# Attention with a gated feed-forward, one core: two constants of the order planner, the sorting of the value groups, and when a group is summed from four copies

## The chip, the core and the metric

The kernel runs on one core of a Trainium2 chip. The metric is the device time of one execution in microseconds (us). Before the change the median of three runs is 769.64 us (769.48 to 770.63).

Five engines work side by side, each with its own queue of instructions, and meet at semaphores: TensorE (PE: matmuls, and PEld: the loading of their weights), VectorE (DVE), ScalarE (ACT), GpSimd (POOL, used only for set-up here) and SyncE (SP, which issues nearly all transfers).

## What is computed

```python
def reference(A_x, A_wqkv, A_wo, B_x, B_w_gate, B_w_up, B_w_down, gate_w):
    x = A_x                                          # 1 x 2048 x 512
    g = _sigmoid((x * gate_w).sum(-1, keepdims=True))
    a = _A_ref(x, A_wqkv, A_wo)                      # attention, 32 heads of 16
    b = _B_ref(x, B_w_gate, B_w_up, B_w_down)        # (silu(x @ w_gate) * (x @ w_up)) @ w_down, width 1792
    return g * a + (1 - g) * b
...
        scores = jnp.einsum("bhqd,bhkd->bhqk", q, k) * (Dh ** -0.5)
        p = _softmax(scores, axis=-1)
        o = jnp.einsum("bhqk,bhkd->bhqd", p, v)
```

Both halves take the same x. All tensors are bf16. The attention has 32 x 2048 x 2048 scores, and an exponential is due for each of them.

## The kernel before

**Tiles.** The queries are cut into 4 blocks of 512, the heads into 8 groups of 4; a block with a group is a unit (32 units, `UNITS`). A unit has 16 key tiles of 128 keys. One key tile of one unit, called a value group `n` here, is 4 heads x 128 keys x 512 queries of scores: 4 matmuls make the scores, their exponentials are taken, and they are multiplied with the values into the PSUM bank `o_ps` of the unit. There are 512 value groups.

**Two ways to take the exponential.** (1) On ScalarE: `emit_pair` (L704) issues two score matmuls into a two-bank tile `s_t`, of which there are two, and one ACT instruction on 128x1024 elements writes `e_t` (10 buffers). Two such pairs make a group. (2) On VectorE: `emit_d` (L774) issues one score matmul into `d_t`, one of three single PSUM banks that it shares with all projections. DVE scales the scores and adds a constant so that the 16-bit result, read as bf16, is a rough exponential (`first`). Four such tiles make the group's 128x2048 tile `y`. The rough exponential is then made better in one of two ways:

- *four summed* (`groups[n] == 4`): three copies of `y`, shifted by constants (`copy`, L816 and after), so that four tiles are multiplied with the values and TensorE's accumulation sums them. DVE does 4 + 3 instructions, TensorE 4 multiplications with the values.
- *two with a product* (`groups[n] == 2`): two bit operations (`bits`) and a multiplication of two 128x2048 tiles (`product`); two tiles are multiplied with the values. DVE does 4 + 2 + 1 instructions, TensorE 2 multiplications with the values.

The tiles `y` and their copies live in 7 homes (`NS`; they are named `c_t`, and the seventh lies in `wd_t` or `kaug` while these are free, so it goes by those names).

**The planner.** The order of every instruction on PE, DVE and ACT is written out by the program as it is built (`ordered` ties each instruction behind the one before on its engine). A planner decides it. It keeps a clock for each engine (`plan.pe`, `plan.dve`, `plan.act`) with a price for each step: an ACT tile 0.9167 us, a round of TensorE 0.217 us, a change between its row-tiled and column-tiled forms 0.107 us, a DVE step some 0.6 us. A round is one of four matmuls that lie side by side in columns of the array (all projections, all multiplications with the values), or the two to four score matmuls that lie side by side in rows. The main loop (L1491) fills the room until the next score tile is free with multiplications with the values (`pv`, from `pv_list`), with pieces of the projections and of the feed-forward (`side`), and, where nothing is left, with time that is counted as spare; then it emits a score pair, on which up to two `d_t` matmuls ride. Some pieces that remain are issued after the last score pair, by `tail_ready` (L1042). `next_pv` forces a multiplication with the values when too many pairs wait (`EB`).

**What the change touches.** `m_free` (L361) says when a single bank can be written again after DVE's read: 0.2 us after the planner's end of that read. The end of `emit_d` (L807) says when DVE can read a `d_t`: 0.28 us after the planner's end of the matmul. `ready` (L813) appends a finished tile of a DVE group to the list `vready`, and `pv_list` (L1330) offers them in that order. `pv` (L902) charges TensorE's clock with the multiplication, from time 0.0 for a DVE tile, that is, without regard to when the tile is ready. `quad` (L1469) chooses how a new DVE group is made: with the product if fewer than two homes (`FREE4`) are free or have a known time of coming free; otherwise four summed if over 0.5 us of TensorE's time has been spare since the last such choice, or if `EAGER` says so; with the product otherwise. `EAGER` is given `back[0]`, the number of ScalarE pairs whose multiplication with the values is still to come. It always says no.

Of the kernel before, what the change touches and what calls it, by code (L numbers as in the profile page):

```python
# [79 lines left out]
def kernel(  # L80
# [215 lines left out]
    plan = Plan()  # L296
    owed = []
    work_at = []
    banks = [0.0] * 3
    held = [None] * 3  # L300

    def spend(mode, mms, ready=0.0):

        plan.seq += 1
        work_at.append((plan.pe, mms))
        plan.pe = max(plan.pe + (FLIP if mode != plan.mode else 0.0), ready) + (0.226 if mode == "F" else 0.217) * mms
        plan.mode = mode
# [16 lines left out]
    def pay(i=0):  # L324
        ready, cost, f, c, key = owed.pop(i)
        spend_v(cost, ready, key)
        keep, plan.chain = plan.chain, None
        f()
        plan.chain = keep
        if c is not None:  # L330
            c.owed -= 1
            if c.done():
                c.done_at = plan.slot
# [14 lines left out]
    def m_tile(name, ride=None):  # L348
        while m_ready() is None:
            stuck()  # L350
        i = min((i for i in range(3) if banks[i] is not None), key=lambda i: banks[i])
        if ride is None:
            plan.pe = max(plan.pe, banks[i])
        else:
            ride.append(max(plan.pe - ROUND, banks[i]) + ROUND)
            plan.pe = max(plan.pe, ride[0])
        banks[i] = None
        held[i] = ps_m[i].tile([P, QBW], F32, tag=f"m{i}", name=name)
        return held[i]

    def m_free(ps, t):  # L361
        i = [h is ps for h in held].index(True)
        banks[i], held[i] = t + 0.2, None

    def emit_piece(c):
        mms, f = c.pieces[c.i][:2]
# [317 lines left out]
    vready = []  # L684
# [4 lines left out]
    def score(ps, b, rows=64):  # L689
        n, j = b // 4, HEADS[b % 4]  # L690
        (qb, g), kt = UNIT[n // KT], n % KT
        r = slice(32 * j // rows * rows, 32 * j // rows * rows + rows)
        q = (q0a if n < KT // 2 else q0[qb])[r, j % 2, :] if g == 0 else get_q(qb, g)[r, j % 2, :]
        mm(ps, lhsT=kaug[r, g, kt * P:(kt + 1) * P], rhs=q, start=True, stop=True,
           tile_position=(r.start, 0))
# [4 lines left out]
    e_end = {}  # L700
# [38 lines left out]
    d_wait = []  # L739
# [15 lines left out]
    def take_home():  # L755
        i = min(range(NS), key=lambda i: c_free[i])
        t, c_free[i] = c_free[i], 1e9
        assert t < 1e9
        users[i] = [1, 0.0]
        return i, t  # L760

    def home(i=None, t=0.0):

        if i is None:
            i, t = take_home()
        plan.dve = max(plan.dve, t)
        if i < NS - 1:
            return i, vex.tile([P, NV * QBW], U16, tag=f"h{i}", name="c_t", bufs=1)[:, :]
        return i, (kaug[:, 0, :] if au > QB else wd_t[:, 0:4, :].rearrange("p f d -> p (f d)")).bitcast(U16)
# [4 lines left out]
    def emit_d(i, rows=32, riding=False):  # L774
        if not vcur:
            n = v_take()
            waiting[n] = [NV, None, take_home()]
            vcur.update(n=n, left=list(range(NV)), y=None)
            y_live[0] += 1
        n, left, cur = vcur["n"], vcur["left"], waiting[vcur["n"]]  # L780
        left.remove(i)
        end = []
        d_t = m_tile("d_t", end if riding else None)
        score(d_t[:, :], 4 * n + i, rows)
        if not left:
            vcur.clear()

        def first():
            if cur[1] is None:
                cur[1] = home(*cur[2])  # L790
            h, y = cur[1]
            vec.tensor_scalar(out=y[:, i * QBW:(i + 1) * QBW], in0=d_t[:, :], scalar1=EXP_A, scalar2=EXP_B[groups[n]],
                              op0=ALU.mult, op1=ALU.add)
            m_free(d_t, plan.dve)
            cur[0] -= 1
            if cur[0]:
                return
            plan.last = ("y", n)
            if groups[n] == 2:
                vops.extend([(0.6, lambda: bits(n, 0, y), ("y", n), n, True), (0.6, lambda: bits(n, 1, y), None, n, True),  # L800
                             (MUL_US, lambda: product(n, h, y), None, n, False)])
            else:
                users[h][0] = 2
                ready(n, 0, h, y)
                for k in range(1, 4):
                    vops.append((0.6, lambda k=k: copy(n, k, h, y), ("y", n) if k == 1 else None, n, True))
        d_wait.append(((end[0] if end else plan.pe) + 0.28, first, n))  # L807

    waiting = {}
    copies = {}  # L810
    part = {}

    def ready(n, k, h, c):  # L813
        copies[n, k] = (c.bitcast(BF16), h)
        vready.append((plan.dve + 0.3, n, k))

    def copy(n, k, i, y):
        h, c = home()
        vec.tensor_scalar(out=c, in0=y, scalar1=SHIFTS[k - 1], scalar2=None, op0=ALU.add)
        ready(n, k, h, c)  # L820
        if k == 3:
            drop(i, plan.dve + 0.2)
            y_live[0] -= 1

    def bits(n, k, y):
        h, c = home()
        if k == 0:
            vec.tensor_scalar(out=c, in0=y, scalar1=0x007F, scalar2=0x3F00, op0=ALU.bitwise_and, op1=ALU.bitwise_or)
            part[n] = (h, c)
        else:  # L830
            vec.tensor_scalar(out=c, in0=y, scalar1=0xFF80, scalar2=None, op0=ALU.bitwise_and)
            ready(n, 0, h, c)

    def product(n, h, y):
        i, c = part.pop(n)
        vec.tensor_tensor(out=c.bitcast(BF16), in0=y.bitcast(BF16), in1=c.bitcast(BF16), op=ALU.mult)
        ready(n, 1, i, c)
        drop(h, plan.dve + 0.2)
        y_live[0] -= 1
# [62 lines left out]
    def pv(n, k=None, most=QBW):  # L902

        un = n // KT
        c0 = cut.pop("done", 0)
        c1 = min(QBW, c0 + most)
        cols = slice(c0, c1)
        if un not in o_of:
            while un and un - 1 not in osbs:
                pay()  # L910
            plan.pe = max(plan.pe, o_end[0])
            o_of[un] = ps_o.tile([P, QBW], F32, tag="o", name="o_ps")
        if v_of(n) is not None:
            force(v_of(n))
        o = o_of[un]
        first = pvs[un] in ((0, KT // 2) if un == 0 else (0,))
        last = un == 0 and pvs[un] == KT // 2 - 1 or pv_left(un) == 1
        if k is not None:
            c, slot = copies[n, k]
        for i, b in enumerate(range(4 * n, 4 * n + 4)):  # L920
            j = HEADS[i]
            v0 = (4 * UNIT[un][1] + j) * VC
            e = e_of[b] if k is None else c[:, i * QBW:(i + 1) * QBW]
            mm(o[32 * j:32 * j + 32, cols], lhsT=vaug[:, n % KT, v0:v0 + 32], rhs=e[:, cols],
               start=first, stop=last, tile_position=(0, 32 * j), skip_group_check=True)
        share = (c1 - c0) / QBW
        if c1 < QBW:
            cut.update(item=(n,) if k is None else (n, k), done=c1)
            spend("C", share, 0.0 if k is not None else max(e_end[b] for b in range(4 * n, 4 * n + 4)))
            return  # L930
        cut.clear()
        if k is not None:
            copies.pop((n, k))
        else:
            for b in range(4 * n, 4 * n + 4):
                e_of.pop(b)
                e_left.pop(b, None)
        pvs[un] += 1
        if un == 0 and pvs[0] == KT // 2:
            later(0.6, take_part, plan.pe + 0.47)  # L940
        spend("C", share, 0.0 if k is not None else max(e_end.pop(b, 0.0) for b in range(4 * n, 4 * n + 4)))
        if k is None:
            done_a[un] += 1
        else:
            done_v[un] += 1
            drop(slot, plan.pe + 0.2)
# [257 lines left out]
    for qb in range(1, QB):  # L1204
        d = qb * KT
        q, bd = q0_pieces(qb)
        q = pace.add(q, 0, d - 13, [known])
# [3 lines left out]
    for qb in range(QB):  # L1211
        for b in range(NB):
# [18 lines left out]
            q = pace.add(q_pieces(qb, b), rel, d - QLEAD, after)  # L1231
# [229 lines left out]
    def v_take():  # L1461
        un = v_unit()
        hi[un] -= 1
        n = un * KT + hi[un]
        groups[n] = 2 if quad() else 4
        forward()
        return n

    def quad():  # L1469
        if sum(f < 1e9 for f in c_free) < FREE4:  # L1470
            return True
        if spare[0] > SPARE or EAGER(len(GQL()), back[0]):
            spare[0] = 0.0
            return False
        return True
    FREE4 = 2
    EAGER = lambda q, b: False
    GQL = lambda: []
    back = [0]

# [10 lines left out]
    while au < UNITS:  # L1491
# [45 lines left out]
        n = au * KT + at_  # L1537
# [56 lines left out]
    for tq in range(TQ):  # L1594
        t = (QB - 1) * TQ + tq
# [39 lines left out]
```

## Time and profile before

| | us |
|---|---|
| median of three runs | 769.64 |
| the profiled execution, its own time | 769.63 |
| its span, from first to last instruction | 767.9 |
| start of the first ACT score tile (`e_t`) | 13.86 |
| start of the last one | 758.70 |
| ACT score tiles / `th` tiles of the feed-forward | 780 / 56 |

Busy shares of the span: PE 95%, DVE 96%, ACT 98%. The granted TensorE clock is 1.00 in all stretches. Read the profile so: the busy share of PE counts a matmul from its start to its modelled end, about 384 ns for 512 columns, though the next one starts after 0.22 us; so the starts of the matmuls in the timeline tell how much room PE has, and the busy share does not. The same holds in part for ACT and DVE: an ACT score tile is shown with some 1.1 us and the next one starts 0.90 us after it.

### The profile page before, as it was taken

How to read it: one execution, taken by the hardware profiler on the slowest of the kernel's cores; microseconds unless marked ns; L12 is line 12 of the kernel's file. 1: busy time of each engine (PE TensorE's matmuls, PEld its weight loads, DVE VectorE, ACT ScalarE, POOL GpSimd, SP SyncE). 2: the span in 40 equal slices, each digit the busy share in tenths (PEclk: the TensorE clock that was granted, in tenths of full speed). 3: DMA queues.
4: the chain of work that ended last, by engine and by line, in shares of the span. 5: the costliest groups of instructions: out<-in, count | busy, mean ns of one | idle time of the engine just before them, and what ended most of it. 6: DMA issues, size and time to landing. Idle time of an engine off the chain costs nothing.

```text
span 767.9 us, 22047 instructions
## 1 busy us (share of the span) xinstructions
PE 733.1 (95%) x9044; PEld 221.6 (29%) x9045; DVE 738.8 (96%) x1213; ACT 752.5 (98%) x849; POOL 10.6 (1%) x25
## 2 busy tenths in 40 slices
PE   8999999999999999999999999999999999999997
PEld 3323222222222222223322222223222322222222
DVE  6889999999999999999999999999999999999994
ACT  5999999999999999999999999999999999999996
POOL 5000000000000000000000000000000000000000
PEclk9999999999999999999999999999999999999999
DMA  8002304134200113220100230311000232100001
GB/s 192 2 5 50 73 15 85 31 107 101 57 19 13 32 24 78 60 52 22 37 26 12 49 84 20 75 34 41 20 12 26 60 77 59 31 16 16 16 28 35
DMA packets 91020, 34.38 MB, mean 45 GB/s; under 512 B 75488, under 2 KB 90472, under 8 KB 90920
## 3 DMA queue, kind: packets, MB, share of 16 engines
q1 hardware_dynamic: 89192, 32.66, 17.8%
q8 instruction: 70, 1.15, 0.6%
q10 hardware_dynamic: 1728, 0.33, 0.2%
q14 instruction: 30, 0.25, 0.1%
HBM read 21.55 MB, written 2.35 MB: 31 GB/s over the span
## 4 chain that ended last, share of the span: by engine, by line
ACT 32%; PE 30%; DVE 28%; issue 8%; DMA 1%; SPq 1%; DVEq 0%; ACTq 0%
ACT e_t L167 30%; DVE c_t L176 17%; PE s_t L164 10%; PE o_ps L164 8%; PE gu L164 6%; DVE kaug L176 3%; PE ops L164 3%; DVE mt L176 2%; DVE gs L176 2%; ACT th L167 1%; DVE on L176 1%; PE qp L164 1%; DVE osb L176 1%; PE warm L164 1%; SPq L176 1%
## 5 line engine op out<-in xcount | busy, mean ns | idle before, releaser
L167 ACT ACTIVATE e_t<-s_t 128x1024 bf16<-128x1024 f32 x780 | 728.3, 1105 | 1.3 <-PE s_t L164 0.7
L176 DVE TENSOR_SCALAR c_t<-d_t 128x512 uint16<-128x512 f32 x420 | 275.3, 681 | 2.2 <-PE d_t L164 2.0
L164 PE MATMUL s_t<-qx,kaug 32*128 32x512 bf16 (+1 forms) x1228 | 239.0, 384 | 16.1 <-ACT e_t L167 14.0
L164 PEld LDWEIGHTS <-kaug 32*128 32x128 bf16 (+1 forms) x2048 | 88.7, 91 | 321.8 <-issue 317.6
L164 PE MATMUL o_ps<-e_t,vaug 128*32 128x512 bf16 (+2 forms) x1608 | 154.2, 379 | 0.0
L176 DVE TENSOR_SCALAR c_t<-c_t 128x2048 uint16<-128x2048 uint16 x212 | 142.0, 683 | 1.7 <-PE o_ps L164 1.4
L164 PE MATMUL d_t<-qx,kaug 32*128 32x512 bf16 x404 | 131.9, 383 | 0.0
L164 PE MATMUL o_ps<-c_t,vaug 128*32 128x512 bf16 (+2 forms) x1244 | 111.3, 370 | 2.6 <-DVE osb L176 2.1
L164 PEld LDWEIGHTS <-vaug 128*32 128x32 bf16 x3048 | 68.8, 94 | 107.2 <-issue 95.2
L164 PE MATMUL gu<-xT,wg 128*32 128x512 bf16 x896 | 73.0, 384 | 0.0
L164 PE MATMUL gu<-xT,wu 128*32 128x512 bf16 x896 | 68.3, 382 | 0.2 <-DVE c_t L176 0.2
L176 DVE TENSOR_TENSOR c_t<-c_t 128x2048 bf16<-128x2048 bf16 x50 | 60.7, 1213 | 0.0
L164 PE MATMUL ops<-wd_t,mt 128*32 128x512 bf16 x672 | 57.5, 382 | 0.0
L164 PE MATMUL s_t<-q,kaug 32*128 32x512 bf16 (+1 forms) x196 | 38.2, 383 | 5.8 <-ACT e_t L167 5.4
L176 DVE TENSOR_SCALAR kaug<-d_t 128x512 uint16<-128x512 f32 x60 | 39.6, 680 | 0.0
L176 DVE SCALAR_TENSOR_TENSOR mt<-gs,gu 128x512 bf16<-128x512 bf16 x56 | 38.1, 680 | 1.5
L176 DVE SCALAR_TENSOR_TENSOR gs<-th,gu 128x512 bf16<-128x512 bf16 x56 | 38.0, 678 | 0.5 <-ACT th L167 0.5
L167 ACT ACTIVATE th<-gu 128x512 bf16<-128x512 f32 x56 | 37.7, 673 | 0.0
L164 PEld LDWEIGHTS <-mt 128*32 128x32 bf16 (+1 forms) x1037 | 24.5, 95 | 28.6 <-issue 22.0
L164 PEld LDWEIGHTS <-wu 128*32 128x32 bf16 x896 | 19.5, 95 | 25.4 <-issue 17.6
L164 PEld LDWEIGHTS <-wg 128*32 128x32 bf16 x896 | 17.8, 94 | 26.0 <-issue 23.2
L176 DVE TENSOR_SCALAR kaug<-c_t 128x2048 uint16<-128x2048 uint16 x33 | 22.5, 681 | 0.1
(141 smaller groups left out, 444.7 us busy)
## 6 DMA issues: line engine op xcount, KB each, us to landing
wg<-in_B_w_gate_dram SPq DMA_DIRECT2D x56, 128.0 KB
wu<-in_B_w_up_dram SPq DMA_DIRECT2D x56, 128.0 KB
on<-osb SPq DMA_DIRECT2D x120, 16.0 KB
rb<-rr SPq DMA_DIRECT2D x15, 128.0 KB
wd_t<-in_B_w_down_dram SPq DMA_DIRECT2D x7, 256.0 KB
qx<-qst SPq DMA_DIRECT2D x96, 16.0 KB
qx<-aq SPq DMA_DIRECT2D x96, 16.0 KB
out_dram<-o_t SPq DMA_DIRECT2D x12, 128.0 KB
```

Of the source, the lines that this page charges most:

```text
L164: return ordered(nc.tensor.matmul(*args, **kw))
L167: ordered(nc.scalar.activation(*args, **kw))
L176: return lambda *a, **kw: ordered(f(*a, **kw))
```

## The change

The two constants go from 0.2 to 0.14 and from 0.28 to 0.25. A new function `usable` keeps `vready` sorted by the time from which a tile is ready and notes that time; `pv` charges TensorE's clock for a DVE tile from that time on instead of 0.0. `EAGER` says yes where at most three ScalarE pairs wait.

```diff
     def m_free(ps, t):
         i = [h is ps for h in held].index(True)
-        banks[i], held[i] = t + 0.2, None
+        banks[i], held[i] = t + 0.14, None
...
-        d_wait.append(((end[0] if end else plan.pe) + 0.28, first, n))
-
+        d_wait.append(((end[0] if end else plan.pe) + 0.25, first, n))
+
+    def usable(t, n, k):
+        vready.append((t, n, k))
+        vready.sort(key=lambda v: v[0])
+        ready_at[n, k] = t
+
+    ready_at = {}
...
     def ready(n, k, h, c):
         copies[n, k] = (c.bitcast(BF16), h)
-        vready.append((plan.dve + 0.3, n, k))
+        usable(plan.dve + 0.3, n, k)
...
-            spend("C", share, 0.0 if k is not None else max(e_end[b] for b in range(4 * n, 4 * n + 4)))
+            spend("C", share, ready_at[n, k] if k is not None else max(e_end[b] for b in range(4 * n, 4 * n + 4)))
...
-        spend("C", share, 0.0 if k is not None else max(e_end.pop(b, 0.0) for b in range(4 * n, 4 * n + 4)))
+        spend("C", share, ready_at[n, k] if k is not None else max(e_end.pop(b, 0.0) for b in range(4 * n, 4 * n + 4)))
...
-    EAGER = lambda q, b: False
+    EAGER = lambda q, b: b <= 3
```

## Prediction, made before the changed kernel ran

> **What bounds the kernel now.** I read the page's totals first, then the busy time by stage, the waits of TensorE, and the timeline for the pace of each engine. From the page:
>
> ```profile
> PE 733.1 (95%) x9044; PEld 221.6 (29%) x9045; DVE 738.8 (96%) x1213; ACT 752.5 (98%) x849; POOL 10.6 (1%) x25
> ...
> L167 ACT ACTIVATE e_t<-s_t 128x1024 bf16<-128x1024 f32 x780 | 728.3, 1105 | 1.3 <-PE s_t L164 0.7
> L176 DVE TENSOR_SCALAR c_t<-d_t 128x512 uint16<-128x512 f32 x420 | 275.3, 681 | 2.2 <-PE d_t L164 2.0
> ...
> L176 DVE TENSOR_SCALAR c_t<-c_t 128x2048 uint16<-128x2048 uint16 x212 | 142.0, 683 | 1.7 <-PE o_ps L164 1.4
> ...
> L176 DVE TENSOR_TENSOR c_t<-c_t 128x2048 bf16<-128x2048 bf16 x50 | 60.7, 1213 | 0.0
> ```
>
> By stage (window; busy PE, PEld, DVE, ACT):
>
> ```profile
> 240.00:320.00 80.00, 77.15 (x952) 23.14 (x944) 79.86 (x129) 79.97 (x92) 0.00 (x0) 1.00 0.15 38
> 480.00:560.00 80.00, 78.04 (x974) 22.59 (x966) 79.76 (x128) 79.89 (x92) 0.00 (x0) 1.00 0.18 41
> ```
>
> and the waits of TensorE:
>
> ```profile
> PE s_t L164 <- ACT e_t L167: 20.3, 60, 0.7
> ...
> PE o_ps L164 <- DVE osb L176: 2.1, 5, 0.9
> ```
>
> ACT is the last limit: busy without a gap, and what TensorE waits for is ACT giving back a score tile. But three engines lie within a few per cent, so each one's real pace is needed. The timeline gives it by starts. TensorE:
>
> ```profile
> 301.62 0.40 PE L164 MATMUL o_ps<-c_t,vaug 128*32 128x512 bf16 x4
> 301.84 0.39 PE L164 MATMUL o_ps<-e_t,vaug 128*32 128x512 bf16 x4
> 302.17 0.39 PE L164 MATMUL s_t<-qx,kaug 64*128 64x512 bf16 x2
> 302.49 0.40 PE L164 MATMUL o_ps<-c_t,vaug 128*32 128x512 bf16 x4
> ```
>
> A column round after a column round: 0.22 us. A change to the score form: 0.33 and back 0.32. Over the whole trace the medians are 0.222 and 0.3215, so a change of form costs 0.10 on top of a round. DVE:
>
> ```profile
> 302.77 0.68 DVE L176 SCALAR_TENSOR_TENSOR gs<-th,gu 128x512 bf16<-128x512 bf16 x1
> 303.37 0.68 DVE L176 TENSOR_SCALAR c_t<-d_t 128x512 uint16<-128x512 f32 x1
> ...
> 308.09 1.22 DVE L176 TENSOR_TENSOR c_t<-c_t 128x2048 bf16<-128x2048 bf16 x1
> 309.22 0.68 DVE L176 SCALAR_TENSOR_TENSOR mt<-gs,gu 128x512 bf16<-128x512 bf16 x1
> ```
>
> One step is 0.60, a product 1.13. On ACT, 394 of the 721 intervals between neighbouring score tiles are 0.903 or 0.904 us, which is its own pace (0.9035); a `th` tile takes 0.477. From the first score tile's start (13.86) to the last one's (758.70) is 744.84 us; ACT's own need there is 779 x 0.9035 + 56 x 0.477 = 730.5. The difference, 14.3 us, is ACT starting late, nearly always because its score matmuls came late: call it ACT's loss, 0.018 us a tile.
>
> **The change, part by part.** The order of the two built programs, counted by operation, says what happens.
>
> *Groups.* DVE groups go from 122 to 124, so ACT tiles from 780 to 776: 4 x 0.9035 = 3.6 us less for ACT. Groups with a product go from 78 to 30, four summed from 44 to 94. DVE: 48 products less (48 x 1.13 = 54.2), bits and copies from 288 to 342 (54 x 0.60 = 32.4 more), 8 first steps more (4.8): 17.0 less. TensorE: value rounds for DVE groups from 78 x 2 + 44 x 4 = 332 to 30 x 2 + 94 x 4 = 436, for ACT's from 390 to 388, and 3 filler rounds fall away: 99 x 0.222 = 22.0 more; changes of form from 1500 to 1515, 1.5 more; 4 score pairs less, 0.9. Sum +22.6 us. Eight more `d_t` matmuls ride with score pairs and start within 0.01 us of them, at nothing. Transfers are the same in number; SP's queue only swaps weight loads with neighbours.
>
> *What TensorE's load does to ACT.* Priced with 0.222 and 0.10, TensorE's work up to the last score tile is 693.0 us before, 37.5 under ACT's 730.5, and 714.0 after (1.6 of the added work lies behind that tile), 12.9 under ACT's 726.9. That cover is what hides the added rounds; it is not gone, but thin. To see what thin cover costs I cut the program before into 49 windows of 16 score tiles and set each one's room (ACT's own need less TensorE's priced work, per tile) beside ACT's measured loss in it. Fifths by room: room 0.001, 0.027, 0.050, 0.071, 0.101 us; loss 0.0168, 0.0167, 0.0178, 0.0187, 0.0224. So loss did not grow as room fell, down to none. After, the mean room falls from 0.049 to 0.017; 22 of 49 windows are below zero, by 3.8 us in all, against 4 windows and 0.4 us. Where room is negative, the loss is at least the deficit, and a share of TensorE's stalls on DVE comes on top (all stalls in starts that a DVE read or write ended: 8.5 us, 0.011 a tile). Taking the larger of the usual 0.0175 and that floor, window by window, gives 1.7 us more than now; taking the fifths alone gives 0.8 less. I take +0.9, the nearer to the floor, since both are observed but the negative windows are new. Upper bound: deficits paid on top of the usual loss (3.8) with as much again from DVE stalls that no longer find cover: +7.6.
>
> *The Trainium skill on this.* "Perfetto Trace Analysis" (Identifying the Most-Contended Engine) holds that the busy time of matmuls is no measure of TensorE's headroom and that the busy share of weight loading is to be looked at instead. By that share, 29% here, TensorE would be far from a limit and the added 22.6 us would cost nothing. The starts above agree that 95% means little, but price 693.0 of 730.5 as taken, which is no headroom of 71%.
>
> *Constants and sorting.* The new values are what the trace has: a single bank is written again at the earliest 0.054 us after DVE's 0.68 us read ends, 0.135 after that read's pace of 0.60; DVE starts a `d_t` at the earliest 0.457 after its matmul's start, 0.24 after the 0.217 round. So nothing waits in principle, but a margin of 0.06 is gone: at 26 places where TensorE already stalls on such a bank it could cost 0.06 each, 1.6 us. Against that DVE is relieved by 17.0 us, and 1.6 us of ACT's loss stands behind a stall on DVE. The sorting and the honest charge in `pv` move multiplications off tiles that are not there yet; TensorE's waits for `c_t` sum to 1.3 us by starts. Bounds -1.6 to +1.6; I take -0.3, the relief being the larger row.
>
> *The end.* One thing in the new order is plain loss. A column tile of the output projection slips behind the last score pair: 28 matmuls, 7 rounds, stand now between it and the first matmuls of the tail. Before:
>
> ```profile
> 758.00 0.39 PE L164 MATMUL s_t<-qx,kaug 64*128 64x512 bf16 x2 [0.53 <-ACT e_t L167]
> 758.91 0.81 PE L164 MATMUL al<-wo_t,on 128*128 128x512 bf16 x2 [0.53 <-ACT e_t L167]
> 759.65 0.62 PE L164 MATMUL o_ps<-e_t,vaug 128*32 128x512 bf16 x8
> 760.32 0.69 ACT L167 ACTIVATE osb<-o_ps,tiny 128x512 bf16<-128x512 f32 x1 [0.54 <-PE o_ps L164]
> ```
>
> `al` waited for a score bank until 0.91 after the last score pair, and the last value round came when ACT's last tile was done. With 7 rounds ahead, `al` starts 0.32 + 7 x 0.222 + 0.10 = 1.97 after the pair: 1.06 later, and the rest of the tail hangs on it (value rounds, `osb`, denominators, output). Some of it hides only if TensorE is early at the pair, all 1.6 us of the rounds show if it is late; bounds 0.6 to 1.6; I take 1.1.
>
> Sum: 769.6 (the profiled execution, 769.63, equal to the median 769.64) - 3.6 + 0.9 - 0.3 + 1.1 = 767.7 us. About 0.2% (1.5 us, so 768.1 and 771.2) is what can be told from no change.
>
> **Rivals.**
>
> 1. *TensorE has headroom*: room never decides, ACT's loss goes by the fifths alone, and the relieved DVE stalls less. 769.6 - 3.6 - 0.8 - 0.3 + 1.1 = 766.0. For it: the flat loss in the fifths. Against: 22 windows where TensorE's priced work is over ACT's. (It is what the rule of the Trainium skill's "Perfetto Trace Analysis" named above would lead to.)
> 2. *The gain is eaten.* Each window with negative room pays its deficit on top of the usual loss: +3.8. 769.6 - 3.6 + 3.8 - 0.3 + 1.1 = 770.6, no change. For it: TensorE can only be one score tile ahead, so usual loss and deficit may add. Against: the lowest fifth shows no sum.
> 3. *Slower: TensorE becomes the bound in the second half.* In stretches of 48 score tiles TensorE's work now meets or passes ACT's at tiles 240-288 (44.0 us to 43.8), 384-480 (89.8 to 89.2) and 528-624 (88.4 to 88.1). There every stall on DVE is ACT's loss. It decides where room per tile is under those stalls, 0.011 us. Price +3.8 and, with all the stalls of the negative windows, +3.8 more: 774.4; with half of the latter 772.5. Against it: today TensorE waits for ACT's score tiles for 20.3 us by the page and 34.1 us by starts, and the added work is 22.6.
>
> That the groups do not change is excluded by the built order.
>
> **How the numbers follow.** Forecast 0.40 (its own range 766.8 to 768.9, a quarter of it within 0.2%), rival 1 0.12, rival 2 0.20, rival 3 0.28. Faster 0.30 + 0.12 = 0.42; the same 0.10 + 0.20 = 0.30; slower 0.28. The range takes rival 1 and most of rival 3, whose upper end is left out: 765.9 to 773.0.
>
> **What would show it.** Right: 776 score tiles at 0.9035; the waits of `s_t` for ACT down from 20.3 to some 5 to 10 us; PE busy near 750, DVE near 722; first to last score tile about 742; a run of 7 `ops` rounds behind the last score pair and `al` 2 us after it. Wrong: ACT idle on PE in the middle stretches, or a loss over 0.022 us a tile there (rival 3); a loss under 0.017 (rival 1); an end no longer than before.

## The result and the profile after

The changed kernel takes 766.74 us (median of 6 runs, 765.88 to 767.69) against 769.42 (6 runs, 769.09 to 770.63): ratio 0.9964, 95% interval 0.9951 to 0.9976. That is 2.7 us faster, clear of 0.2%; the forecast was 767.7. One execution of run e9 (1059.84 us at a granted clock of 0.56) and one of the kernel before beside it (2632.69 us) are left out below.

The two profiled executions, taken apart. *Need* is what ACT's tiles take at their own pace (0.9035 us from one score tile to the next, 0.477 for a `th`) between the starts of the first and the last score tile; *loss* is what that stretch takes beyond the need; *end* runs from the last tile's start to the last instruction.

| us | before | after | difference | forecast |
|---|---|---|---|---|
| start of the first score tile | 13.86 | 12.77 | -1.09 | 0 |
| ACT's need (780 and 776 tiles) | 730.5 | 726.9 | -3.6 | -3.6 |
| ACT's loss | 14.3 | 14.0 | -0.3 | +0.9 - 0.3 |
| end | 9.2 | 10.5 | +1.3 | +1.1 |
| span | 767.9 | 764.2 | -3.75 | |
| the execution's own time | 769.63 | 765.88 | -3.75 | |

The first line is not the change: up to there the two orders are the same, and in the profiled executions below, which share them too, the first tile starts anywhere from 12.4 to 13.9. Its size is about the gap between these two executions (-3.75) and the medians (-2.7).

The page after, in the lines that answer to those shown of before:

```profile
PE 742.6 (97%) x9472; PEld 218.8 (29%) x9473; DVE 725.0 (95%) x1227; ACT 748.5 (98%) x845; POOL 10.6 (1%) x25
...
L167 ACT ACTIVATE e_t<-s_t 128x1024 bf16<-128x1024 f32 x776 | 724.4, 1089 | 1.2 <-PE s_t L164 0.7
L176 DVE TENSOR_SCALAR c_t<-d_t 128x512 uint16<-128x512 f32 x444 | 292.8, 684 | 7.8 <-PE d_t L164 7.0
...
L176 DVE TENSOR_SCALAR c_t<-c_t 128x2048 uint16<-128x2048 uint16 x249 | 167.2, 685 | 0.7 <-PE o_ps L164 0.2
...
L176 DVE TENSOR_TENSOR c_t<-c_t 128x2048 bf16<-128x2048 bf16 x23 | 28.0, 1217 | 0.0
```

DVE is 13.8 us less busy and now waits for `d_t` (7.0 us) where it hardly did; TensorE is 9.5 us busier by records, although 22.6 us of work came by starts: the rest went into time that the records already counted. By stage, and in the waits of TensorE:

```profile
240.00:320.00 80.00, 79.58 (x1022) 22.63 (x1020) 79.62 (x135) 80.00 (x91) 0.00 (x0) 1.00 0.14 36
480.00:560.00 80.00, 78.66 (x1012) 22.86 (x1008) 78.25 (x132) 79.86 (x91) 0.00 (x0) 1.00 0.17 41
```

```profile
PE s_t L164 <- ACT e_t L167: 11.9, 35, 1.0
...
PE gu L164 <- DVE c_t L176: 0.5, 2, 0.3
```

ACT is as full as before. TensorE's waits for ACT fell from 20.3 to 11.9 us, and the 2.1 us for `osb` are gone. By starts, TensorE's stalls that ended with a read or write of DVE in the loop fell from 8.5 to 2.5 us.

The end of the changed kernel:

```profile
753.21 0.39 PE L164 MATMUL s_t<-qx,kaug 64*128 64x512 bf16 x2
...
753.53 1.70 PE L164 MATMUL ops<-wd_t,mt 128*32 128x512 bf16 x28
...
755.15 0.82 PE L164 MATMUL al<-wo_t,on 128*128 128x512 bf16 x2
...
756.58 0.69 ACT L167 ACTIVATE osb<-o_ps,tiny 128x512 bf16<-128x512 f32 x1 [1.85 <-PE o_ps L164]
```

The 28 `ops` matmuls (7 rounds) stand behind the last score pair, `al` starts 1.94 us after the pair (0.91 before), and ACT sits 1.85 us (0.54 before) until the last values are there.

### The profile page after: what moved, and what is told of

It reads as the page before. It is cut to its first block, busy times and chain, and to the rows that moved or that the text cites. A ratio compares the mean times of both kernels' runs of the same rounds, so it can differ in the third digit from the quotient of the medians.

```text
span 764.2 us, 22889 instructions
## 1 busy us (share of the span) xinstructions
PE 742.6 (97%) x9472; PEld 218.8 (29%) x9473; DVE 725.0 (95%) x1227; ACT 748.5 (98%) x845; POOL 10.6 (1%) x25
## 4 chain that ended last, share of the span: by engine, by line
PE 41%; ACT 37%; DVE 13%; issue 8%; DMA 1%; SPq 0%; ACTq 0%; DVEq 0%
ACT e_t L167 35%; PE s_t L164 14%; PE o_ps L164 13%; DVE c_t L176 7%; PE gu L164 5%; PE ops L164 3%; PE qp L164 2%; ACT th L167 2%; DVE mt L176 2%; DVE gs L176 1%; DVE kaug L176 1%; PE vp L164 1%; PE dps L164 1%; PE kp L164 1%; PE warm L164 1%
## 5 line engine op out<-in xcount | busy, mean ns | idle before, releaser
L176 DVE TENSOR_SCALAR c_t<-d_t 128x512 uint16<-128x512 f32 x444 | 292.8, 684 | 7.8 <-PE d_t L164 7.0
L164 PE MATMUL s_t<-qx,kaug 32*128 32x512 bf16 (+1 forms) x1224 | 238.2, 384 | 11.8 <-ACT e_t L167 10.8
L164 PEld LDWEIGHTS <-kaug 32*128 32x128 bf16 (+1 forms) x2048 | 81.9, 91 | 322.9 <-issue 319.8
L176 DVE TENSOR_SCALAR c_t<-c_t 128x2048 uint16<-128x2048 uint16 x249 | 167.2, 685 | 0.7 <-PE o_ps L164 0.2
L164 PE MATMUL o_ps<-c_t,vaug 128*32 128x512 bf16 (+2 forms) x1548 | 135.7, 374 | 0.2 <-DVE c_t L176 0.2
L164 PEld LDWEIGHTS <-vaug 128*32 128x32 bf16 x3476 | 72.0, 95 | 108.7 <-issue 94.9
L176 DVE TENSOR_SCALAR kaug<-d_t 128x512 uint16<-128x512 f32 x52 | 34.5, 682 | 0.4 <-PE d_t L164 0.2
L176 DVE TENSOR_SCALAR kaug<-c_t 128x2048 uint16<-128x2048 uint16 x46 | 31.5, 686 | 0.1
L176 DVE TENSOR_TENSOR c_t<-c_t 128x2048 bf16<-128x2048 bf16 x23 | 28.0, 1217 | 0.0
L164 PEld LDWEIGHTS <-wu 128*32 128x32 bf16 x896 | 19.6, 95 | 23.9 <-issue 15.6
L176 DVE TENSOR_SCALAR c_t<-kaug 128x2048 uint16<-128x2048 uint16 x37 | 24.9, 686 | 0.3 <-PE o_ps L164 0.2
```

What stands on the lines that cost most here:

```text
L164: return ordered(nc.tensor.matmul(*args, **kw))
L176: return lambda *a, **kw: ordered(f(*a, **kw))
```

## Experiments

Each run has a profile and is timed beside the kernel before on the same chip. The terms of the profiled executions, the changed kernel's among them:

| run | score tiles | loss, us | of it in tiles 22 to 700 | end, us | median, us | ratio to before, 95% interval |
|---|---|---|---|---|---|---|
| before | 780 | 14.3 | 11.5 | 9.2 | 769.42 | |
| changed kernel | 776 | 14.0 | 11.4 | 10.5 | 766.74 | 0.9964 [0.9951, 0.9976] |
| e1 constants | 778 | 16.2 | 13.2 | 9.1 | 769.57 | 1.0004 [0.9995, 1.0013] |
| e2 four summed | 778 | 15.9 | 12.7 | 11.2 | 770.30 | 1.0018 [1.0009, 1.0026] |
| e3 clean end | 776 | 13.8 | 11.3 | 9.2 | 765.27 | 0.9949 [0.9936, 0.9961] |
| e4 before, TensorE loaded | 780 | 23.3 | 19.7 | 9.2 | 777.82 | 1.0113 [1.0099, 1.0127] |
| e5 before, DVE light | 780 | 13.4 | 10.2 | 9.2 | 767.55 | 0.9976 [0.9966, 0.9985] |
| e6 after, DVE heavy | 776 | 29.8 | 25.9 | 10.5 | 782.25 | 1.0167 [1.0154, 1.0181] |
| e7 before, load planned | 780 | 17.4 (15.9) | 14.8 (13.3) | 10.2 | 772.76 | 1.0044 [1.0032, 1.0057] |
| e8 tighter | 774 | 17.2 (15.6) | 14.3 (12.7) | 9.1 | 765.02 | 0.9944 [0.9932, 0.9957] |
| e9 bank and four summed | 774 | 15.6 | 12.7 | 10.8 | 765.93 | 0.9967 [0.9954, 0.9980] |
| e10 clean end, old constants | 778 | 15.4 | 12.7 | 9.2 | 768.10 | 0.9987 [0.9978, 0.9995] |
| e11 another plan | 776 | 15.7 | 12.5 | 9.2 | 766.51 | 0.9966 [0.9954, 0.9978] |
| e12 another plan | 776 | 16.9 (15.6) | 14.1 (12.8) | 9.2 | 768.24 | 0.9988 [0.9979, 0.9996] |

Two things in the loss are not the plan's. First, all these orders are the same on TensorE up to the 23rd score tile, yet the first 21 tiles lose 1.50 to 2.07 us, so one column leaves them out, and the tiles from 701 on, where orders that are the same up to there (the changed kernel and e3; e2 and e10) go apart. Second, in the profiled executions of e7, e8 and e12 TensorE's granted clock is halved for 3.41 us in mid-run. In e12 (the last figures are the granted clock, the DMA share and GB/s):

```profile
208.60:212.00 3.40, 3.40 (x29) 0.65 (x28) 2.63 (x4) 2.93 (x4) 0.00 (x0) 0.50 0.40 89
```

There a column round takes 0.35 to 0.40 us, not 0.22, and ACT loses 1.4 to 1.7 us; the figures in brackets are without that, but for the usual 0.018 us a tile. Of e12's eleven executions nine have a mean clock of 0.995 to 0.998 and take 767.7 to 769.5 us; the two at 1.000 take 766.5 and 767.0. Its median is no measure of its plan.

### The parts of the change (e1, e2, and the sorting)

The sorting needed no run. With both new constants and the new `EAGER`, the built order without `usable` and without the charge in `pv` is the changed kernel's, instruction by instruction on PE, DVE, ACT and SP; it is the same with either of the other parts alone, and without them it gives the order of before. This part of the change moves nothing.

```diff
-        banks[i], held[i] = t + 0.2, None
+        banks[i], held[i] = t + 0.14, None
...
-        d_wait.append(((end[0] if end else plan.pe) + 0.28, first, n))
+        d_wait.append(((end[0] if end else plan.pe) + 0.25, first, n))
```

> The kernel before with the two constants alone (0.14 and 0.25). Its built order has 778 ACT score tiles, two fewer than before, 79 groups with a product and 44 four summed, and the end as before. Theory (the gain is ACT tiles removed, the loss per tile does not move): 2 x 0.9035 = 1.8 us less, 767.6 where before is 769.4, ratio 0.9977, loss near 14.2 us. Rival (the constants act by shorter or longer stalls on the single banks): away from that by up to 1.6 us either way. Rival (the constants bring the whole gain and the rest is idle): 766.7.

No gain: 1.8 us of need went, 1.9 us of loss came. The theory failed in its second half. TensorE's stalls on DVE, by starts, are 8.1 us against 8.5, so the lost margin of 0.06 us at each bank is not what cost it.

```diff
-    EAGER = lambda q, b: False
+    EAGER = lambda q, b: b <= 3
```

> The kernel before with the choice of four summed groups alone. 778 ACT score tiles, 19 groups with a product and 104 four summed, TensorE's priced work 27 us up; behind the last score pair stand 11 column rounds. Theory: -1.8 us by ACT tiles, and the end longer by 11 x 0.222 + 0.42 - 0.91 = 1.95 us: about 769.6, no change, loss 14 to 16 us. Rival (the tighter cover of TensorE costs its deficits, 3.9 us, on top): 773. Rival (four summed groups are what brings the gain by relieving DVE): 767 or less.

The end is 1.95 us longer to the hundredth of what 11 rounds were priced at, need is 1.8 less, loss 1.6 more: slightly slower. So neither part alone is faster; both together let the planner make one group more than either (776 tiles), with a loss of 14.0. Where the loss comes from is therefore what had to be found.

### The end (e3)

```diff
-    EAGER = lambda q, b: b <= 3
+    EAGER = lambda q, b: b <= 3 and vu < UNITS - 3
```

> The changed kernel, but with the four summed choice closed to new groups of the last three units, so that no column round stands behind the last score pair. 776 ACT score tiles, 37 groups with a product and 87 four summed. Theory (those 7 rounds cost the end 1.1 to 1.3 us, since the tail's first matmuls wait for them): 766.7 - 1.2 = 765.5, the time from the last score tile's start to the end 9.2 us as before the change. Rival (the end hides them, and 10.5 us is due to something else): 766.7.

```profile
752.99 0.39 PE L164 MATMUL s_t<-qx,kaug 64*128 64x512 bf16 x2
...
753.67 0.81 PE L164 MATMUL al<-wo_t,on 128*128 128x512 bf16 x3 [0.29 <-ACT e_t L167]
...
755.08 0.69 ACT L167 ACTIVATE osb<-o_ps,tiny 128x512 bf16<-128x512 f32 x1 [0.54 <-PE o_ps L164]
```

As the theory had it: with nothing between, `al` follows 0.68 us after the pair, ACT waits 0.54 again, the end is 9.2 us, and the time falls by 1.5 us against the changed kernel. Its median is below that of both kernels; its ratio's interval still overlaps that of the changed kernel.

### Does TensorE's load cost, and where (e4, e7)

```diff
+        doses[0] += 1
+        if doses[0] % 8 == 0 and not last and un:
+            for j in range(4):
+                mm(o[32 * j:32 * j + 16, :], lhsT=vaug[:, 0, G * 4 * VC:], rhs=xT[:, 0, 0:QBW],
+                   start=False, stop=False, tile_position=(0, 32 * j), skip_group_check=True)
         cut.clear()
```

> The kernel before with 84 added filler rounds on TensorE (one behind every eighth multiplication with the values, adding zeros; 18.6 us by 0.222), unknown to the planner, so that TensorE's room under ACT falls from 38 to 20 us and nothing else changes. Theory (ACT's loss does not depend on room as long as windows are not below zero by much; floor estimate 16.7 against 13.8): 769.4 to 772.3. Rival (deficits of the windows, 4.5 us, come on top of the usual loss): 773.5. Rival (TensorE has headroom): 769.4.

All three expectations were too low: +8.6 us, loss 23.3, for 84 rounds, with 20 us of room still left over the whole. One of the added rounds, in the timeline of TensorE in this run:

```profile
306.55 0.39 PE L164 MATMUL s_t<-qx,kaug 32*128 32x512 bf16 x2
306.55 0.39 PE L164 MATMUL d_t<-qx,kaug 32*128 32x512 bf16 x1
306.87 0.62 PE L164 MATMUL qp<-xT,wqk 128*32 128x512 bf16 x8
307.31 0.39 PE L164 MATMUL o_ps<-e_t,vaug 128*32 128x512 bf16 x4
307.53 0.39 PE L164 MATMUL o_ps<-xT,vaug 128*16 128x512 bf16 x4
307.85 0.39 PE L164 MATMUL s_t<-qx,kaug 64*128 64x512 bf16 x2
```

The added round (`o_ps<-xT`, 307.53) is the fourth between two score pairs: the pairs lie 1.30 us apart where ACT needs 0.90, and ACT starts that tile 0.28 us late. TensorE can be ahead by one score tile only, so the room of quieter stretches is not there to be used. By the built order, priced as in the prediction, 72 of the 87 filler rounds (3 were there before) stand in intervals between two score pairs that are longer than ACT's own.

```diff
                    start=False, stop=False, tile_position=(0, 32 * j), skip_group_check=True)
+            spend('C', 1)
```

> The kernel before with the same rule of filler rounds as in the loaded run (one behind every eighth multiplication with the values), now charged to the planner's clock, so that it plans around them. 780 ACT score tiles as before; groups with a product 87, four summed 35; TensorE has 63 column rounds and 20 changes of form more than before in all (16 us); 3 rounds behind the last score pair. Theory B (where the rounds stand decides, not how many): within 1.5 us of before, 769 to 771, against +8.6 for the unplanned ones. Rival (a round costs what it costs, 0.1 us each as in the loaded run): 775 or more.

Between the two: +3.5 us, of which the profiled execution shows 1.0 as a longer end (`ops` rounds and some of `a_l` stand behind the last score pair) and 3.1 as loss, with a first tile 1.2 earlier; 1.5 of the 3.1 is the stretch at half the clock, so some 1.6 is left for the rounds (1.8 by tiles 22 to 700). With the planner told, 43 of 84 filler rounds stand in intervals over 0.1 us longer than ACT's, and 7 in intervals 0.02 longer. So both rivals fail as stated: planned load is not free (some 0.03 us of loss for each of the 63 rounds more, and the longer end), but loses a third of what unplanned load does (0.10). TensorE's room is thus no headroom that any round may use: of 18.6 us of unplanned rounds 8.6 came out as time, of 16 us of planned work 3.5. The page of the loaded run:

```profile
PE 744.1 (96%) x9381; PEld 224.3 (29%) x9381; DVE 742.4 (96%) x1213; ACT 759.1 (98%) x849; POOL 10.6 (1%) x25
```

Weight loading stands at 29%, and at 28 or 29% in every run here, while each added round cost a tenth of a microsecond. The rule of the Trainium skill that the prediction weighed ("Perfetto Trace Analysis", Identifying the Most-Contended Engine) is right here that the busy share of matmuls says little. Of the two measures that it names instead, the share of weight loading does not show this limit either; the other, the share of peak arithmetic, was not worked out.

### Does DVE's load cost (e5, e6)

```diff
-        vec.tensor_tensor(out=c.bitcast(BF16), in0=y.bitcast(BF16), in1=c.bitcast(BF16), op=ALU.mult)
+        vec.tensor_tensor(out=c[:, 0:1664].bitcast(BF16), in0=y[:, 0:1664].bitcast(BF16), in1=c[:, 0:1664].bitcast(BF16), op=ALU.mult)
```

> The kernel before, its order untouched, with the product of each of its 78 groups taken over 1664 of 2048 columns (the last 384 columns of one of the two tiles stay without their factor, so the result is not the reference's). DVE has 78 x 0.21 = 16.6 us less to do, about what the change took from it; TensorE and ACT have the same work in the same order. Theory A (a relieved DVE is why ACT's loss stayed at 14 us though TensorE had 99 rounds more: its stalls on DVE fell from 8.5 to some 3 us by starts): ACT's loss falls from 14.3 to 9 to 12 us, 765 to 767.5 where before is 769.3. Theory B (the planner puts added rounds only where there is room, DVE's load does not matter): no change, 769.3 within 0.7.

The time falls by 1.8 us (interval 1.2 to 2.6), with TensorE and ACT untouched. Of that 0.9 is seen as loss in the profiled execution, 1.3 by tiles 22 to 700. TensorE's stalls on DVE fell to 3.6 us by starts, as theory A has it, and it waits longer for ACT instead:

```profile
PE s_t L164 <- ACT e_t L167: 24.9, 75, 0.7
```

So DVE's relief is worth 1 to 2 us, less than theory A's 2 to 5.

```diff
         vec.tensor_scalar(out=c, in0=y, scalar1=SHIFTS[k - 1], scalar2=None, op0=ALU.add)
+        again2[0] += 1
+        if again2[0] % 10 == 0:
+            vec.tensor_scalar(out=c, in0=y, scalar1=SHIFTS[k - 1], scalar2=None, op0=ALU.add)
```

> The changed kernel, its order untouched, with every tenth of the shifted copies written twice (28 copies, 16.9 us more on DVE, which takes the relief back). Theory A: ACT's loss rises from 14.0 by 3 to 6 us, 770 to 773 where the changed kernel is 766.7. Theory B: 766.7 to 768 (the copies come at places that the planner does not know of, so a little is to be paid).

+15.5 us for 16.9 us of DVE work: nearly one for one, far over both. The waits of this run:

```profile
PE o_ps L164 <- DVE c_t L176: 4.3, 16, 0.4
...
ACT e_t L167 <- PE s_t L164: 3.7, 13, 0.5
ACT e_t L167 <- PE d_t L164: 2.8, 11, 0.4
```

A copy that is 0.6 us late holds up a multiplication with the values, and TensorE, in order, holds up the score pair behind it. That DVE is 95% busy and idles some 7 us for `d_t` in the changed kernel does not mean that it has 0.6 us to spare at a given place. Nor has DVE become the limit as a whole: at its pace by starts its work in e6 is some 720 us (an estimate from the intervals between its instructions) of the 756.7 between the first and the last score tile. The relief of e5 and the burden of e6 are of the same size and move the time by unlike amounts; that the order fits the one and not the other is the likely reason, and no run takes it apart.

### How much of the loss is the plan (e8 to e12)

e8 is e3 with 0.12 for the bank, e9 the changed kernel with 0.28 for the score tile, e10 is e3 with 0.2 and 0.28, e12 is e3 with 0.15 for the bank. e11 moves one due time:

```diff
-            c = pace.add((out_pieces if pos else down_pieces)(qb, tq), rel, a0 + per * (0.64 + 0.36 * (tq + 1) / TQ),
+            c = pace.add((out_pieces if pos else down_pieces)(qb, tq), rel, a0 + per * (0.64 + 0.36 * (tq + 1) / TQ) - (16 if pos == QB - 1 else 0),
```

> The changed kernel with the clean end (four summed choice closed to the last three units) and the bank constant at 0.12, below the 0.135 that the trace shows. 774 ACT score tiles, 35 groups with a product and 90 four summed. By tiles alone: 1.8 us under the clean-end run, 763.5. Floor estimate of the loss 18.0 against 15.3: 766. Rival (a constant below the traced one makes TensorE stall on the banks at each use): 768 or more.

774 tiles and 765.02: the saved tile pair was mostly taken back by loss (12.7 against e3's 11.3 in tiles 22 to 700, without the stretch at half the clock), so it is level with e3. TensorE's stalls on DVE are 3.1 us, so the constant below the traced 0.135 did not make it stall at each use.

> The changed kernel with the score-tile constant back at 0.28: the bank constant 0.14 and the four summed choice stay. 774 ACT score tiles, 31 groups with a product and 94 four summed, 9 column rounds behind the last score pair (end longer by 9 x 0.222 + 0.42 - 0.91 = 1.5 us). Theory C (ACT tiles count 0.9 us each, the loss scatters between 14 and 17 us from plan to plan and has no bearing on the constants): 769.3 - 5.4 + 1.5 + (0 to 2.9) = 765.4 to 768.3. Theory D (the score-tile constant is what brought the loss from 15.9 to 14.0): loss 16 or more, so 767 to 768.3.

> The changed kernel with both constants back (0.2 and 0.28) and the clean end (four summed choice closed to the last three units). 778 ACT score tiles, 27 groups with a product and 96 four summed. From the run with the four summed choice alone (770.3) less its longer end (1.95): 768.3, loss 15.9. Theory C allows a loss of 14 to 17: 766.5 to 769.5. Against the clean-end run with the new constants (765.3) this prices the constants: 1.8 us by tiles, the rest by loss.

> The changed kernel with the due times of the last block's output tiles 16 slots earlier, and nothing else: another plan of the same rules, 776 ACT score tiles, 33 groups with a product and 91 four summed, no column round behind the last score pair. If the loss is a matter of the rules: 14 us, 765.3 as the clean-end run. Theory C: loss 14 to 17, 765.3 to 768.3.

> The changed kernel with the clean end and the bank constant 0.15 instead of 0.14: 776 ACT score tiles, 33 groups with a product and 91 four summed, no column round behind the last score pair. If the loss is a matter of the rules: 14 us, 765.3. Theory C: loss 14 to 17, 765.3 to 768.3.

e9 and e10 came inside theory C, and e10 where its sum was (768.3). In e9 the loss is 15.6 where theory D asked for 16 or more, and the time is 765.93 where it asked for 767 or more. e11 decides: with both constants as in the changed kernel and only one due time moved, the loss is 15.7 (12.5 in tiles 22 to 700, against 11.4). Theory C holds in this: the loss belongs to the single plan. The changed kernel and e3 share their order on TensorE up to score tile 710 and lose 11.4 and 11.3 us in tiles 22 to 700; e2 and e10, on two chips, share theirs up to 711 and lose 12.7 each. As profiled, the whole losses of these eight runs scatter over 13.8 to 17.2 us; without the stretches at half the clock over 13.8 to 15.9. And it is not even: the plan of the changed kernel and e3 stands alone at 11.3 to 11.4, the five others with the four summed choice lie at 12.5 to 12.8. What makes this one plan better by some 1.2 us stays open.

## Why the prediction was right

**How near.** 766.74 lies just under the forecast's own range (766.8 to 768.9), and nearer to rival 1 (766.0) than to the forecast (767.7). The stated range, 765.9 to 773.0, took in rivals of opposite sign, so it tells little of the working; the terms do.

**The bound and the tiles.** ACT sets the pace before and after, and four tiles less were worth 3.6 us: -3.6 by the count, at a pace that did not move. (Of the 721 intervals before, 435 are 0.903 or 0.904 us; the 394 of the prediction are those whose score matmuls came over 0.54 us ahead.) e1, e2 and e10 (two tiles less each) and e8, e9 (six) carry the same need in their sums.

**The end.** 1.1 was taken, 1.26 is measured; e3 removes it by removing the rounds, and e2 has 1.95 for 11 rounds.

**The loss.** The sum had +0.6, measured -0.3: this term is most of the 1.0 us between forecast and result. The step that failed is the reading of the fifths, "loss did not grow as room fell, down to none": true of windows that the planner had filled, but it says nothing of what a round costs that is put elsewhere. In e4 the room fell from 38 to 20 us and the loss rose by 9.0; in e7, with the planner told, by some 1.6. So room over 16 tiles does not decide, and the place of a round does. That the number of intervals longer than ACT's is the measure of it is not shown: priced as in the prediction they are 215 before, 233 after and 234 in e7, with 11.5, 11.4 and 13.3 us lost in tiles 22 to 700. In the change, three things met: the planner laid its 99 rounds with a view to room; DVE's relief gave back 1 to 2 us (e5); and this plan came out 1.1 to 1.4 us better than the five others of its rules. Without the stretches at half the clock the eight runs with the four summed choice (the changed kernel, e2, e3, e8 to e12) have a mean loss of 15.2, 0.9 over the kernel before, which is close to the +0.6 of the sum; by that mean the changed kernel would have been at about 767.9, at the edge of 0.2% from before. So +0.6 is near what plans of these rules show on the mean, though its working does not give the reason, and that this plan is 1.2 us better still is luck. How the 14.0 divides among the three stays open.

**The constants.** Their price was sought in the wrong place, 26 stalls of 0.06 us. Neither e1 nor e8 has more stalls of this kind. What they do is let the planner fit another group in: two tiles, 1.8 us, in e1 lost again to the plan, and between e10 and e3 worth 2.8 us by the medians (in the profiled executions 1.8 by tiles and 1.6 by loss, the latter being the plan's: e11, with the constants of e3, has a loss of 15.7).

**The sorting.** That it moves multiplications "off tiles that are not there yet" was wrong: it moves nothing.

**The rivals.** TensorE's headroom (766.0) is refuted by e4 and e7, though the time came nearer to it than to the forecast. That deficits are paid on top (770.6) and that TensorE becomes the bound in the second half (772.5 to 774.4) did not happen in this plan; e4 and e6 show that both dangers are real for work that the order has no place for.

**The signs named.** `s_t` waits 11.9 us (5 to 10 said), PE busy 742.6 (750), DVE 725.0 (722), first to last tile 740.9 (742), `al` 1.94 us after the pair (2).

## What to carry to other kernels

Where three engines are as close as here (95, 96 and 98% busy) and one can be ahead by a single tile, slack summed over a stretch is not slack: price each interval between two tiles of the bounding engine, and ask of every added instruction which interval it lands in. When a planner writes the order, a change of one constant replaces the whole plan: separate what is counted (tiles, rounds at the end) from what scatters, by running a few neighbouring plans, before a gain is put down to the rule that was changed, and compare the same stretch of tiles at the same granted clock. And look at what the new plan leaves behind the last tile: seven rounds there cost 1.3 of the 3.6 us gained.

## What was not expected of the hardware

The start of the first score tile scatters by 1.5 us (12.4 to 13.9) between profiled executions that share the instructions up to it; for a change of 3 us that is to be taken out before profiles are compared. The granted clock can fall to half for 3.41 us in mid-run (e7, e8, e12), with 1.4 to 1.7 us of ACT's time lost; in e8 TensorE was idle by no more than 0.3 us at a time in the 2 us before, and no row shows why. Of ACT's intervals whose score matmuls came over 0.54 us ahead, most are 0.903 or 0.904 us, but 36 before and 20 after are 0.920, and no row shows why.
